# Maximum of three products as one product plus a clipped maximum of two difference products

## The chip, the cores and the metric

The kernel runs on one core of a Trainium2 chip. The metric is the device time of one execution in microseconds (us). The engines are called as in the profile: PE is the matrix engine (PEld its weight loads), DVE the vector engine, ACT the scalar engine, POOL GpSimd, SP the sync engine, which here issues loads and stores. The kernel has two parts in one launch: a gated linear attention, and behind it a feed-forward layer whose hidden values are a maximum of three products.

## The reference, cut to what matters

```python
# q, k, v, alpha: (4, 8, 768, 48) float32; w1, w2, w3: (384, 768); w_out: (768, 384)
for t in range(S):
    state = alpha[:, :, t, :, None] * state + einsum('bhd,bhe->bhde', k[:, :, t], v[:, :, t])
    y[:, :, t] = einsum('bhd,bhde->bhe', q[:, :, t], state)
x = y.transpose(0, 2, 1, 3).reshape(3072, 384)
h = np.maximum(np.maximum(x @ w1, x @ w2), x @ w3)
out = h @ w_out                                     # (3072, 384) float32
```

## The kernel before

**Groups.** The 3072 tokens are worked on in 12 groups of 256 (`n`; NG = 12, TG = 256). A group is two blocks of 128 tokens of one batch entry. Its attention takes two units `u`, four heads each; the feed-forward layer `ffn(n)` takes the whole group.

**Attention of a group.** SP loads a (alpha), q, k and v (`load`, L371) into one of five sets of buffers. `decay` makes logarithms of the decays on ACT (L402, L407; the product of two neighbouring decays before that is L398, on POOL for all but the first group). `prep` sums them with matmuls (L465, L468), takes exponentials on ACT (L473, L475), multiplies q and k by these (L482, mostly POOL) and scales v to f16 (L494). PE transposes q and k (L508), DVE copies them (L516), PE makes the scores (L528) and DVE masks them (L537). `state` sums the states (L560; L573, L579 and L447 carry them on), `output` adds the part from the state (L596) and from the scores (L617), ACT scales the result (L630), and PE turns it into `xT` (L638), which DVE (L649) or ACT (L645) copies. `xT`, f16, has x transposed: features on partitions, 256 tokens along the free axis, with 12 buffers, one per group.

**Feed-forward layer of a group.** `grow` takes two of the six blocks of 128 hidden features (`j`) and one of three weights (`g`): six matmuls of 128x128 weights with 256 columns of xT (L668), into one bank of PSUM. The first weight's product is copied to `hT` by ACT (L676); the second and third are taken in by DVE, as a maximum of the bank and hT (L680). `shrink` then multiplies six blocks of hT by Wout for each block of 128 tokens, 384 columns each (L692), ACT copies the result (L700) and SP stores it (L703). hT has three buffers, and the output four.

**Weights.** POOL's queue loads W1, W2 and W3 into `wcat` and Wout into `wo16`, turning them to f16 on the way (`weights`, L382). Each transfer has a gate, a step of the attention that must have come first (`WAFTER`): the first after v of unit 1, the second after v of unit 2, the third after k of unit 3, Wout after k of unit 5.

**What sets the order.** Nothing is scheduled by the compiler. Each piece of work is a step of a `Plan`, with its engine, an estimated cost, a rank, what it reads and writes and which of the eight PSUM banks it needs. `order` works through a list schedule on these estimates, with a model of the transfers: of all steps whose inputs, engine and banks are free, the one that can start earliest goes next, and the lower rank decides between equals. Attention steps have ranks near 2n, those of `ffn(n)` begin at 1.9n + 5.5. The instructions are then written in that order; each engine carries out its own in order and waits for what really has or has not come.

Of the kernel before, what the change touches and what calls it, by code (L numbers as in the profile page):

```python
# [10 lines left out]
FP32 = mybir.dt.float32  # L11
FP16 = mybir.dt.float16

AOP = mybir.AluOpType
AFT = mybir.ActivationFunctionType
# [6 lines left out]
NBANKS = 8  # L22
# [207 lines left out]
def kernel(  # L230
# [12 lines left out]
    nc = tc.nc  # L243

    B, H, S, D = q.shape
    NT, DM = out.shape
    DF = moe_w_out.shape[0]
    BH = B * H
    P = 128
# [4 lines left out]
    NFT = DM // P  # L254
    NJ = DF // P
    NU = NCB * B
    UB = 2
# [26 lines left out]
    sb = ctx.enter_context(tc.tile_pool(name="sb", bufs=1))  # L284
# [6 lines left out]
    ident, maskA, order = d16[:, :P], d16[:, P:3 * P], d16[:, 3 * P:]  # L291
# [7 lines left out]
    def homes(n, shape, dtype, name):  # L299
        return [sb.tile(shape, dtype, name=f"{name}{i}") for i in range(n)]  # L300
# [18 lines left out]
    e12s = homes(6, [P, NP, UB, 2], FP32, "e")  # L319
    G0s = homes(2, [P, NP], FP32, "G")  # L320
    G1s = homes(2, [P, NP], FP32, "H")
    wcat = sb.tile([P, NFT, 3, DF], FP16, name="wcat")
    wo16 = sb.tile([P, NJ, DM], FP16, name="wo16")
    for t in las:
        nc.vector.memset(t[:, :, :, D:], 0.0)
# [3 lines left out]
        for t in zz:  # L329
            nc.gpsimd.memset(t, 0.0)  # L330

    plan = Plan({x: range(NBANKS) for x in ("Lp", "hp", "tp", "A", "yp", "xp", "pp", "gp", "op")})
    place = {}

    psall = pspool.tile([P, NBANKS, 512], FP32, name="psum")
# [1 line left out]
    def bank(key, shape, dtype):  # L337
        n = int(np.prod(shape[1:]))
        flat = psall[:, place[key], :].bitcast(dtype) if dtype != FP32 else psall[:, place[key], :]
        if len(shape) == 3:  # L340
            return flat[:, :n].rearrange("p (a b) -> p a b", a=shape[1])
        if len(shape) == 4:
            return flat[:, :n].rearrange("p (a b c) -> p a b c", a=shape[1], b=shape[2])
        return flat[:, :n]
# [5 lines left out]
    live = {}  # L350
# [3 lines left out]
    LEAD = 5.5  # L354
    WAFTER = {2: (0,), 4: (1,), 7: (2,), 11: (3,)}
    SLOPE = 1.9
# [8 lines left out]
    def load(n, lo, hi, names="aqkv"):  # L365
        c, b = divmod(n, B)
        for x in names:
            t = ld[x][n % NL]

            def run(x=x, t=t):  # L370
                nc.sync.dma_start(t[:, lo:hi].rearrange("p h r d -> p h (r d)"),  # L371
                                  views[x][b, c][:, lo:hi])

            plan.step("SP", 0.5, -1.0, run, line="loads",
                      writes=[(x, n % NL, h) for h in range(lo // HH, hi // HH)],
                      load=LOAD * (hi - lo) / H)

    def weights(g, gate):
        w, dst = ((moe_w1, moe_w2, moe_w3, moe_w_out)[g],
                  wo16 if g == 3 else wcat[:, :, g, :])  # L380
        plan.step("POOL", 0.85, -1.0,
                  lambda: nc.gpsimd.dma_start(dst, w.rearrange("(t p) f -> p t f", p=P)),  # L382
                  reads=[gate], writes=[("w", g)], line="weights", load=3.25)


    def decay(n):
# [266 lines left out]
    def ffn(n):  # L653
        c, b = divmod(n, B)
        xT, hT = xTs[n], hTs[n % 3]
        npieces = 3 * (NJ // 2) + UB
        rank = [SLOPE * n + LEAD + SLOPE * i / npieces for i in range(npieces)]
        for j in range(NJ // 2):
            for g in range(3):
                r = rank[3 * j + g]  # L660
                gk = ("gp", n, j, g)

                def grow(j=j, g=g, gk=gk):
                    live[gk] = bank(gk, [P, 2, TG], FP32)
                    for jj in range(2):
                        c0 = (2 * j + jj) * P
                        for kt in range(NFT):
                            nc.tensor.matmul(live[gk][:, jj, :], wcat[:, kt, g, c0:c0 + P],  # L668
                                             xT[:, kt, :], start=(kt == 0), stop=(kt == NFT - 1))

                plan.step("PE", 0.656, r, grow, banks=[gk],
                          writes=[gk] + ([("room", n % 3, j)] if g == 0 else []),
                          reads=[("room", n % 3, j)] * (g > 0) + [("w", g), ("xT", n, 0), ("xT", n, 1)])
                h = hT[:, 2 * j:2 * j + 2, :]
                if g == 0:
                    plan.step("ACT", 0.59, r, lambda h=h, gk=gk: nc.scalar.copy(out=h, in_=live[gk]),  # L676
                              reads=[gk], writes=[("hT", n % 3, j)])
                else:
                    plan.step("DVE", 0.69, r,
                              lambda h=h, gk=gk: nc.vector.tensor_max(h, live[gk], h),  # L680
                              reads=[gk, ("hT", n % 3, j)], writes=[("hT", n % 3, j)])
        for i in range(UB):
            m = n * UB + i
            r = rank[3 * (NJ // 2) + i]
            ok = ("op", m)
            parts = [(0, NJ)] if n < NG - 1 else [(0, NJ - 2), (NJ - 2, NJ)]
            for lo, hi in parts:
                def shrink(i=i, ok=ok, lo=lo, hi=hi):
                    if lo == 0:
                        live[ok] = bank(ok, [P, DM], FP32)  # L690
                    for kt in range(lo, hi):
                        nc.tensor.matmul(live[ok], hT[:, kt, i * P:(i + 1) * P], wo16[:, kt, :],  # L692
                                         start=(kt == 0), stop=(kt == NJ - 1))

                plan.step("PE", 0.1627 * (hi - lo), r + (0.5 if lo else 0.0), shrink,
                          banks=[ok] if lo == 0 else [], writes=[ok, ("ob room", m % 4)],
                          reads=[(x, n % 3, j) for x in ("hT", "room")
                                 for j in range(lo // 2, hi // 2)]
                          + [("w", 3)])
            plan.step("ACT", 0.49, r, lambda m=m, ok=ok: nc.scalar.copy(out=obs[m % 4], in_=live[ok]),  # L700
                      reads=[ok], writes=[("ob", m % 4)])
            plan.step("SP", 0.4, -2.0,
                      lambda i=i, m=m: nc.sync.dma_start(  # L703
                          out[b * S + (2 * c + i) * P:b * S + (2 * c + i + 1) * P, :], obs[m % 4]),
                      reads=[("ob", m % 4), ("ob room", m % 4)], load=0.5)
# [5 lines left out]
    for n in range(NG):  # L711
        if n:
            load(n, 0, H)
        decay(n)
        for u in (2 * n, 2 * n + 1):
            prep(u)
            for j, key in ((2 * u, ("v16", u % NQ)), (2 * u + 1, ("qk", u % NQ, 1))):
                for g in WAFTER.get(j, ()):
                    weights(g, key)
        state(n)  # L720
        output(n)
        if n >= 4:
            ffn(n - 4)
    for n in range(NG - 4, NG):
        ffn(n)
# [35 lines left out]
```

## Time and profile before

| | |
|---|---|
| median of 3 runs | 165.33 us (164.88, 165.33, 165.47) |
| span of the profiled execution | 162.7 us; the runs' own times lie 2.2 to 2.8 us above it |
| PE busy | 146.5 us (90%), 2376 matmuls |
| DVE busy | 113.2 us (70%) |
| ACT busy | 84.5 us (52%) |
| POOL busy | 91.6 us (56%) |
| transfers | 26.50 MB, mean 163 GB/s |
| in the chain that ended last | PE 80% (L668 43%, L692 15%), DMA 8%, DVE 3% |

The span runs from the first to the last instruction; the page names no time for the profiled execution apart from the three runs. Busy time of PE counts each matmul to its modelled end, so neighbouring matmuls overlap in it; the spacing of matmuls is read from the chain of waits, where each piece begins when the one before it makes way. A digit of the rows of slices is a tenth of busy time in a fortieth of the span.

### The profile page before, as it was taken

The page shows a single profiled execution, that of the slowest core. Times are in us where ns is not written, and L with a number is a line of the kernel's source. Part 1 is how long each engine was busy: PE and PEld are TensorE (multiplying, and loading weights), DVE is VectorE, ACT ScalarE, POOL GpSimd, SP SyncE. Part 2 cuts the span into 40 slices and gives each one's busy share as a digit, 9 for nine tenths or more (in the row PEclk, how much of TensorE's full clock was granted, in tenths as well). Part 3 has the DMA queues.
Part 4 walks back from the last instruction along what each step waited for, and adds up shares of the span by engine and source line. Part 5 has one row for each costly group of instructions (what it writes and reads, how often), then busy time and mean ns, then how long its engine had stood idle before and what let it go on. Part 6 is the DMA issues. An engine that isn't in the chain of part 4 may idle for free.

```text
span 162.7 us, 5662 instructions
## 1 busy us (share of the span) xinstructions
PE 146.5 (90%) x2376; PEld 116.4 (72%) x2376; DVE 113.2 (70%) x172; ACT 84.5 (52%) x184; POOL 91.6 (56%) x145
## 2 busy tenths in 40 slices
PE   0279588998999999999999999999999999999990
PEld 0247356877787898887688886868868868878770
DVE  3458732899896789989389776558678678836460
ACT  3536327615775685465765755544634725363311
POOL 7087922934729999999569973482872652000000
PEclk9999999999999999999999999999999999999999
DMA  5999999999899989999999902311011020020202
GB/s 132 269 261 264 238 238 209 281 194 266 212 253 257 249 209 246 268 269 301 264 266 263 292 6 77 122 43 64 0 62 39 0 101 4 0 98 2 78 19 97
DMA packets 55880, 26.50 MB, mean 163 GB/s; under 512 B 50608, under 2 KB 55856, under 8 KB 55856
## 3 DMA queue, kind: packets, MB, share of 16 engines
q1 hardware_dynamic: 53440, 23.60, 58.7%
q0 software_dynamic: 1984, 2.36, 8.4%
q8 instruction: 18, 0.29, 0.8%
q10 hardware_dynamic: 432, 0.20, 0.7%
q14 instruction: 6, 0.05, 0.1%
HBM read 23.79 MB, written 4.72 MB: 175 GB/s over the span
## 4 chain that ended last, share of the span: by engine, by line
PE 80%; DMA 8%; DVE 3%; issue 2%; ACT 2%; POOL 2%; SPq 1%; ACTq 0%; DVEq 0%
PE psum L668 43%; PE psum L692 15%; DMA wcat<-in_moe_w_dram 5%; PE psum L528 4%; PE psum L508 4%; PE psum L617 3%; DMA an<-in_alpha_dram 3%; PE psum L638 3%; PE psum L560 3%; PE psum L465 2%; PE psum L596 2%; DVE LA L537 1%; DVE hT L680 1%; PE psum L468 1%; SPq L371 1%
## 5 line engine op out<-in xcount | busy, mean ns | idle before, releaser
L668 PE MATMUL psum<-xT,wcat 128*128 128x256 f16 x648 | 82.0, 276 | 2.0 <-DMA wcat<-in_moe_w_dram 2.0
L668 PEld LDWEIGHTS <-wcat 128*128 128x128 f16 x648 | 61.3, 99 | 10.4 <-DMA wcat<-in_moe_w_dram 2.1
L680 DVE TENSOR_TENSOR hT<-psum,hT 128x512 f16<-128x512 f32 x72 | 49.2, 689 | 23.9 <-PE psum L668 18.1
L676 ACT CAST hT<-psum 128x512 f16<-128x512 f32 x36 | 21.1, 587 | 27.1 <-PE psum L668 26.7
L537 DVE TENSOR_TENSOR LA<-psum,d 128x1024 f16<-128x1024 f32 x24 | 29.2, 1222 | 8.0 <-PE psum L528 7.1
L482 POOL TENSOR_TENSOR qk<-qn,ep 128x384 f16<-128x384 f32 x23 | 22.9, 998 | 17.6 <-ACT ep L473 11.3
L692 PE MATMUL psum<-wo,hT 128*128 128x384 f16 x144 | 26.3, 327 | 0.0
L482 POOL TENSOR_TENSOR qk<-kn,en 128x384 f16<-128x384 f32 x20 | 20.3, 1014 | 0.3
L700 ACT COPY ob<-psum 128x384 f32<-128x384 f32 x24 | 11.4, 478 | 15.1 <-PE psum L692 13.5
L692 PEld LDWEIGHTS <-hT 128*128 128x128 f16 x144 | 13.4, 98 | 7.7
L516 DVE COPY qkT<-psum 128x1024 f16<-128x1024 f16 x24 | 16.3, 683 | 1.9 <-PE psum L508 1.8
L473 ACT ACTIVATE ep<-psum 128x384 f32<-128x384 f32 x24 | 11.9, 494 | 9.9 <-PE psum L465 9.8
L494 POOL TENSOR_SCALAR v<-vn,c 128x384 f16<-128x384 f32 x23 | 13.4, 588 | 6.2 <-DMA vn<-in_v_dram 4.2
L630 ACT ACTIVATE xb<-psum,c 128x384 f16<-128x384 f32 x24 | 12.6, 576 | 5.9 <-PE psum L617 5.9
L465 PE MATMUL psum<-la,c 128*128 128x192 f16 x48 | 10.6, 262 | 5.5 <-ACT la L407 4.8
L447 POOL TENSOR_TENSOR Z<-U,G 48x192 f16<-48x192 f32 x16 | 8.0, 502 | 11.9 <-DVE U L573 11.2
L528 PE MATMUL psum<-qkT 48*64 48x128 f16 x384 | 10.9, 237 | 1.4 <-DVE qkT L516 1.4
L475 ACT ACTIVATE en<-psum 128x384 f32<-128x384 f32 x24 | 11.8, 493 | 0.0
L508 PE MATMUL psum<-d,qk 64*128 64x64 f16 x384 | 10.9, 199 | 0.3 <-POOL qk L482 0.3
L398 POOL TENSOR_TENSOR aa<-an 128x384 f32<-128x384 f32 x11 | 11.0, 1000 | 0.1
L528 PEld LDWEIGHTS <-qkT 48*64 48x64 f16 x384 | 6.7, 114 | 5.3 <-issue 2.4
L649 DVE CAST xT<-psum 128x384 f16<-128x384 f32 x12 | 6.6, 554 | 5.2 <-PE psum L638 5.0
(38 smaller groups left out, 135.8 us busy)
## 6 DMA issues: line engine op xcount, KB each, us to landing
out_dram<-ob SPq DMA_DIRECT2D x24, 192.0 KB, 2.1
an<-in_alpha_dram SPq DMA_DIRECT2D x11, 384.0 KB, 6.5
qn<-in_q_dram SPq DMA_DIRECT2D x11, 384.0 KB, 6.3
kn<-in_k_dram SPq DMA_DIRECT2D x11, 384.0 KB, 6.3
vn<-in_v_dram SPq DMA_DIRECT2D x11, 384.0 KB, 6.5
wcat<-in_moe_w_dram POOLq DMA_DIRECT2D x3, 576.0 KB, 8.2
wo<-in_moe_w_out_dram POOLq DMA_DIRECT2D x1, 576.0 KB, 9.4
an<-in_alpha_dram SPq DMA_DIRECT2D x2, 192.0 KB, 3.9
```

The costliest lines, as they stand in the source:

```text
L465: nc.tensor.matmul(live[Lk][:, :, r, :], tri, la[:, 0, hs, :D], start=True, stop=(r == 1))
L482: nc.gpsimd if eng == "POOL" else nc.vector).tensor_mul(
L494: lambda: nc.gpsimd.tensor_scalar(out=v16, in0=ld["v"][n % NL][:, hs], scalar1=vsc, scalar2=1.0, op0=AOP.mult, op1=AOP.mult),
L508: nc.tensor.transpose(live[tk][:, i, at:at + HALF], qk[rows, w, r, 2 * j:2 * j + 2, :], ident[rows, rows])
L516: lambda: nc.vector.tensor_copy(out=qkT.rearrange("p i w j t -> p i (w j t)"), in_=live[tk]),
L528: nc.tensor.matmul(live[Ak][i * HALF:(i + 1) * HALF, p, at:at + P], qkT[rows, i, 1, j, r * HALF:(r + 1) * HALF], qkT[rows, i, 0, j, :], st ...
L537: lambda: nc.vector.tensor_mul(LA.rearrange("p a j r t -> p (a j) (r t)"), live[Ak].rearrange("p a (j t) -> p (a j) t", j=2), maskA.unsque ...
L630: lambda xb=xb, yk=yk: nc.scalar.activation(out=xb, in_=live[yk].rearrange("p a b -> p (a b)"), func=AFT.Copy, scale=ysc),
L668: nc.tensor.matmul(live[gk][:, jj, :], wcat[:, kt, g, c0:c0 + P], xT[:, kt, :], start=(kt == 0), stop=(kt == NFT - 1))
L676: plan.step("ACT", 0.59, r, lambda h=h, gk=gk: nc.scalar.copy(out=h, in_=live[gk]), reads=[gk], writes=[("hT", n % 3, j)])
L680: lambda h=h, gk=gk: nc.vector.tensor_max(h, live[gk], h),
L692: nc.tensor.matmul(live[ok], hT[:, kt, i * P:(i + 1) * P], wo16[:, kt, :], start=(kt == 0), stop=(kt == NJ - 1))
```

## The change

With W1 in all three products, max(xW1, xW2, xW3) = xW1 + max(0, x(W2 - W1), x(W3 - W1)). The changed kernel makes the differences once, keeps max(0, ...) in hT, and takes xW1 through Wout as x(W1 Wout), where W1 Wout is made once on the chip:

- W1 has a tile of its own, `w1s`; W2 and W3 go to `wcat`, which has two parts now. `differences` subtracts W1 from each in place, in six steps on DVE, two blocks of 128 hidden features each; a grow piece waits for its own step.
- `bypass` transposes W1 on PE (18 blocks, three copies by ACT into `w1T`), multiplies by Wout (18 matmuls, three copies by ACT) and leaves the product in `past`. Both functions are called when the plan has come to group 3, with ranks of 5.0 to 6.5.
- A grow has two weights in place of three. The first product goes through Relu on ACT in place of the copy, the second into the maximum on DVE.
- A shrink begins with three matmuls of xT by `past` in the bank into which hT by Wout is summed. It waits for all of `past`.

```diff
--- before.py
+++ after.py
@@ -319,7 +319,10 @@
     e12s = homes(6, [P, NP, UB, 2], FP32, "e")
     G0s = homes(2, [P, NP], FP32, "G")
     G1s = homes(2, [P, NP], FP32, "H")
-    wcat = sb.tile([P, NFT, 3, DF], FP16, name="wcat")
+    w1s = sb.tile([P, NFT, DF], FP16, name="w1s")
+    w1T = sb.tile([P, NJ, DM], FP16, name="w1T")
+    past = sb.tile([P, NFT, DM], FP16, name="past")
+    wcat = sb.tile([P, NFT, 2, DF], FP16, name="wcat")
     wo16 = sb.tile([P, NJ, DM], FP16, name="wo16")
     for t in las:
         nc.vector.memset(t[:, :, :, D:], 0.0)
@@ -329,7 +332,7 @@
         for t in zz:
             nc.gpsimd.memset(t, 0.0)
 
-    plan = Plan({x: range(NBANKS) for x in ("Lp", "hp", "tp", "A", "yp", "xp", "pp", "gp", "op")})
+    plan = Plan({x: range(NBANKS) for x in ("Lp", "hp", "tp", "A", "yp", "xp", "pp", "gp", "op", "wt", "mp")})
     place = {}
 
     psall = pspool.tile([P, NBANKS, 512], FP32, name="psum")
@@ -377,10 +380,51 @@
 
     def weights(g, gate):
         w, dst = ((moe_w1, moe_w2, moe_w3, moe_w_out)[g],
-                  wo16 if g == 3 else wcat[:, :, g, :])
+                  (w1s, wcat[:, :, 0, :], wcat[:, :, 1, :], wo16)[g])
         plan.step("POOL", 0.85, -1.0,
                   lambda: nc.gpsimd.dma_start(dst, w.rearrange("(t p) f -> p t f", p=P)),
                   reads=[gate], writes=[("w", g)], line="weights", load=3.25)
+
+
+    def differences():
+        for g in range(2):
+            for j in range(NJ // 2):
+                cols = slice(2 * j * P, (2 * j + 2) * P)
+                plan.step("DVE", 0.47, LEAD - 0.5 + 0.5 * g,
+                          lambda g=g, cols=cols: nc.vector.tensor_sub(
+                              wcat[:, :, g, cols], wcat[:, :, g, cols], w1s[:, :, cols]),
+                          reads=[("w", 0), ("w", g + 1)], writes=[("d", g, j)])
+
+
+    def bypass():
+        rank = LEAD + 0.5 * SLOPE
+        for kt in range(NFT):
+            wk = ("wt", kt)
+
+            def turn(kt=kt, wk=wk):
+                live[wk] = bank(wk, [P, NJ, P], FP16)
+                for j in range(NJ):
+                    nc.tensor.transpose(live[wk][:, j, :], w1s[:, kt, j * P:(j + 1) * P], ident)
+
+            plan.step("PE", 0.36, rank, turn, banks=[wk], reads=[("w", 0)], writes=[wk])
+            plan.step("ACT", 0.82, rank,
+                      lambda kt=kt, wk=wk: nc.scalar.copy(
+                          out=w1T[:, :, kt * P:(kt + 1) * P], in_=live[wk]),
+                      reads=[wk], writes=[("w1T", kt)])
+        for kt in range(NFT):
+            mk = ("mp", kt)
+
+            def product(kt=kt, mk=mk):
+                live[mk] = bank(mk, [P, DM], FP32)
+                for j in range(NJ):
+                    nc.tensor.matmul(live[mk], w1T[:, j, kt * P:(kt + 1) * P], wo16[:, j, :],
+                                     start=(j == 0), stop=(j == NJ - 1))
+
+            plan.step("PE", 0.98, rank, product, banks=[mk], reads=[("w1T", kt), ("w", 3)],
+                      writes=[mk])
+            plan.step("ACT", 0.49, rank,
+                      lambda kt=kt, mk=mk: nc.scalar.copy(out=past[:, kt, :], in_=live[mk]),
+                      reads=[mk], writes=[("past", kt)])
 
 
     def decay(n):
@@ -653,11 +697,11 @@
     def ffn(n):
         c, b = divmod(n, B)
         xT, hT = xTs[n], hTs[n % 3]
-        npieces = 3 * (NJ // 2) + UB
+        npieces = 2 * (NJ // 2) + UB
         rank = [SLOPE * n + LEAD + SLOPE * i / npieces for i in range(npieces)]
         for j in range(NJ // 2):
-            for g in range(3):
-                r = rank[3 * j + g]
+            for g in range(2):
+                r = rank[2 * j + g]
                 gk = ("gp", n, j, g)
 
                 def grow(j=j, g=g, gk=gk):
@@ -670,10 +714,13 @@
 
                 plan.step("PE", 0.656, r, grow, banks=[gk],
                           writes=[gk] + ([("room", n % 3, j)] if g == 0 else []),
-                          reads=[("room", n % 3, j)] * (g > 0) + [("w", g), ("xT", n, 0), ("xT", n, 1)])
+                          reads=[("room", n % 3, j)] * (g > 0)
+                          + [("d", g, j), ("xT", n, 0), ("xT", n, 1)])
                 h = hT[:, 2 * j:2 * j + 2, :]
                 if g == 0:
-                    plan.step("ACT", 0.59, r, lambda h=h, gk=gk: nc.scalar.copy(out=h, in_=live[gk]),
+                    plan.step("ACT", 0.59, r,
+                              lambda h=h, gk=gk: nc.scalar.activation(out=h, in_=live[gk],
+                                                                      func=AFT.Relu),
                               reads=[gk], writes=[("hT", n % 3, j)])
                 else:
                     plan.step("DVE", 0.69, r,
@@ -681,22 +728,27 @@
                               reads=[gk, ("hT", n % 3, j)], writes=[("hT", n % 3, j)])
         for i in range(UB):
             m = n * UB + i
-            r = rank[3 * (NJ // 2) + i]
+            r = rank[2 * (NJ // 2) + i]
             ok = ("op", m)
             parts = [(0, NJ)] if n < NG - 1 else [(0, NJ - 2), (NJ - 2, NJ)]
             for lo, hi in parts:
                 def shrink(i=i, ok=ok, lo=lo, hi=hi):
                     if lo == 0:
                         live[ok] = bank(ok, [P, DM], FP32)
+                        for kt in range(NFT):
+                            nc.tensor.matmul(live[ok], xT[:, kt, i * P:(i + 1) * P],
+                                             past[:, kt, :], start=(kt == 0), stop=False)
                     for kt in range(lo, hi):
                         nc.tensor.matmul(live[ok], hT[:, kt, i * P:(i + 1) * P], wo16[:, kt, :],
-                                         start=(kt == 0), stop=(kt == NJ - 1))
-
-                plan.step("PE", 0.1627 * (hi - lo), r + (0.5 if lo else 0.0), shrink,
+                                         start=False, stop=(kt == NJ - 1))
+
+                plan.step("PE", 0.1627 * (hi - lo + (NFT if lo == 0 else 0)),
+                          r + (0.5 if lo else 0.0), shrink,
                           banks=[ok] if lo == 0 else [], writes=[ok, ("ob room", m % 4)],
                           reads=[(x, n % 3, j) for x in ("hT", "room")
                                  for j in range(lo // 2, hi // 2)]
-                          + [("w", 3)])
+                          + [("w", 3)]
+                          + ([("xT", n, i)] + [("past", kt) for kt in range(NFT)]) * (lo == 0))
             plan.step("ACT", 0.49, r, lambda m=m, ok=ok: nc.scalar.copy(out=obs[m % 4], in_=live[ok]),
                       reads=[ok], writes=[("ob", m % 4)])
             plan.step("SP", 0.4, -2.0,
@@ -719,6 +771,9 @@
                     weights(g, key)
         state(n)
         output(n)
+        if n == 3:
+            differences()
+            bypass()
         if n >= 4:
             ffn(n - 4)
     for n in range(NG - 4, NG):
```

## The prediction

> **What bounds the kernel now.** I read the page first: busy shares, the 40 slices, then the chain of waits, the groups by line, and the timelines of TensorE (PE) and GpSimd (POOL) around the first feed-forward matmuls. Whole lines of the page:
>
> ```profile
> PE 146.5 (90%) x2376; PEld 116.4 (72%) x2376; DVE 113.2 (70%) x172; ACT 84.5 (52%) x184; POOL 91.6 (56%) x145
> ...
> PE   0279588998999999999999999999999999999990
> ...
> DMA  5999999999899989999999902311011020020202
> ```
>
> A slice is 4.07 us. PE is full from the eleventh slice (about 41 us) to the end, while the transfers are full only until about 92 us: from 41 us on, what counts is the amount of PE work. The chain of waits says the same, and gives the rates:
>
> ```profile
> 12.53 8.23 DMA wcat<-in_moe_w_dram
> 20.80 1.46 PE psum L668 x6
> ...
> 40.35 1.04 PE psum L692 x6
> ...
> 137.04 0.34 PE psum L638 x6
> ...
> 144.34 6.55 PE psum L668 x60
> 150.89 1.95 PE psum L692 x12
> 152.84 3.93 PE psum L668 x36
> 156.77 1.64 PE psum L692 x10
> 158.48 0.28 ACT ob L700
> ```
>
> Full rates: L668 (x times W1/W2/W3, 256 columns) 6.55/60 = 0.109 us; L692 (times Wout, 384 columns) 1.95/12 = 0.1625 us; L638 (128 columns) 0.34/6 = 0.057 us. The first six L668, behind the landing of W1, took 1.46 us, more than twice the 0.655 us of later: PE is at half speed there. The last PE work ends at 158.4 us; 4.3 us of eviction and store follow, and the change leaves these alone.
>
> The stretch before 41 us decides what the change gives back. PE's timeline there (start, duration, ..., count):
>
> ```profile
> 20.80 1.46 PE L668 MATMUL psum<-xT,wcat 128*128 128x256 f16 x6 [1.96 <-DMA wcat<-in_moe_w_dram]
> 23.52 2.41 PE L668 MATMUL psum<-xT,wcat 128*128 128x256 f16 x12
> 28.05 0.82 PE L668 MATMUL psum<-xT,wcat 128*128 128x256 f16 x6
> 28.87 4.75 PE L668 MATMUL psum<-xT,wcat 128*128 128x256 f16 x42
> ```
>
> POOL's timeline and the view of the tile wcat date the landings:
>
> ```profile
> 18.34 1.59 POOL L382 DMA_DIRECT2D wcat<-in_moe_w_dram  x2
> 30.80 0.89 POOL L382 DMA_DIRECT2D wo<-in_moe_w_out_dram  x1
> ```
> ```profile
> DMA to landing us min/median/max: 8.1/8.2/10.9
> ```
>
> W1 lands at 12.53 + 8.2 = 20.8 us, W2 at 18.34 + 8.1 = 26.4, W3 (issued at 19.2) at 19.2 + 10.9 = 30.1, Wout at 30.8 + 9.4 = 40.2 (9.4 is its row among the DMA issues).
>
> **The change, part by part.**
>
> *Third product gone.* 36 grow pieces of 6 matmuls: 216 x 0.109 = 23.6 us of PE. With them go 36 of the 72 maxima on VectorE (DVE; L680, 689 ns): 24.8 us of DVE. DVE isn't the bound (70%), so that alone is worth nothing.
>
> *Shrink grows.* Three 384-column matmuls more for each of 24 outputs: 72 x 0.1625 = 11.7 us of PE.
>
> *The product W1 Wout.* 18 matmuls of 384 columns: 2.9 us. They need Wout, at 40.2 us, when PE is full: all on the path. The three evictions of 128x384 (478 ns at L700) hide under the next product; the first shrink, which waits for all of them, has other grow pieces beside it.
>
> *Transposes of W1.* 18 of 128 columns; nearest row L638: 18 x 0.057 = 1.0 us, twice that at half speed; the 64x64 transposes of L508 (0.34 us for 16) would make less. They can run from 20.8 us. From there to 26.4 us the changed kernel has no feed-forward matmul to run, so I cost them at nothing; if that cover is gone they cost 1.0 to 2.0 us. ScalarE (ACT) copies each of three 128x768 banks: from 482 ns for 384 and 587 for 512 columns (L645, L676), 0.82 ns a column, so 0.8 us each. Behind them in ACT's queue stands the logarithm L407 of the third group (22.78 us now, there behind an L676 that itself waited 3.2 us); I take that as even.
>
> *Differences.* Six DVE subtractions of 128x768 f16. No row has this form: the f32 128x384 product in SBUF takes 559 ns (L482 on DVE) and L680's 512 columns 689, 1.0 ns a column, which gives 0.94 us for 768; at the rate of the f16 copy L516, 1024 columns in 683 ns, it is 0.51. I take 0.7, the middle. In all 3 to 6 us of DVE, against 24.8 saved. On the path lies the first: the first grow piece now waits for W1, W2 and one subtraction, 26.4 + 0.7 = 27.1 us in place of 20.8. Behind waiting subtractions in DVE's queue stand the copies L516 and the masks L537 of the third group, and behind a waiting grow piece on PE the scores L528 and the rest of the attention.
>
> *Relu in place of the copy at L676.* Same shape, same engine. An Exp of 128x384 takes 494 ns against 482 for a cast: between nothing and 0.02 us each, on an engine that is 52% busy. Nothing.
>
> *Queues.* SP and POOL get no new instruction; the transfers of the weights keep their gates, though the planner may order things anew around them.
>
> *The late start.* By 40.25 us PE has now run 96 L668 (10.5 us): groups 0 and 1, 54 each, are nearly used up, and the third group's xT is copied only at 43.4 us (DVE's timeline). In the changed kernel these two groups hold 72 matmuls (7.9 us), and from 27.1 to 40.25 us are 13.1 us in which to run them and the 3.6 us that a group's attention takes (its pieces in the chain added up). They fit, but there are no more: 24 x 0.109 = 2.6 us of PE work less is done by then, whatever idles. If the third group's attention comes earlier, as a DVE with six maxima fewer by then may let it, this term falls to zero.
>
> *The clock.* The half speed ended at 25.8 us, five us after PE's dense work began. If it lasts five us from 27.1 instead, 2.5 us of work is lost; the window has 13.1 - 11.5 = 1.6 us to spare, so the excess is 0.9, and 2.5 if attention fills that. I take 0, since transposes and attention now fill 20.8 to 27.
>
> The sum: -23.6 + 11.7 + 2.9 + 2.6 = -6.4 us. Against the profiled span, 162.7 becomes 156.3; the span stands 2.6 us below the median of the runs, 165.33, and with the same 2.6 us around it the time is 158.9.
>
> On the clock a rule speaks against this change. The Trainium skill, in "TensorE: Matmul & The Clock Gate" (Part 4, PE-mode transpose), says that the full clock doesn't engage for transposes, because they don't count as PE activity; by it the transposes between 20.8 and 27 us would do nothing for the first grow pieces, and the sum would be -6.4 + 2.5, or 161.4 us. The trace bears out the half speed (1.46 against 0.655 us) but has no such transposes.
>
> **The rivals.**
>
> *A late and slow start.* PE stays at half speed until 32 us or so (2.5 us) and the transposes are not hidden (up to 1.0): 158.9 + 2.5 to 3.5, some 161.8. For it: PE was busy 7.8 us between 10 and 20 us without leaving half speed, since that work had gaps. Against it: the attention of the second group fills much of 20.8 to 27 in any case, at half speed all the more.
>
> *The gap costs nothing.* Attention takes the place of the early grow pieces, the third group's xT comes by about 37 us: 165.33 - 9.0 = 156.3. For it: L528 at 22.19 us stood behind the L668 that waited 1.96 us for W1. Against it: v of the third group was issued at 16.06 us and landed 14.5 us later (DMA issues of that stretch), at 30.6, which bounds how early that attention can be.
>
> *A blocked queue.* Orders are written from planned landings, and W1's came at least 1.96 us later than planned. If all six subtractions stand in DVE's queue ahead of the third group's copies and wait for W3, grow pieces and attention start near 31 us: four us more, and the cold start's 2.5 on top undo the 6.4: 165.3, on either side of no change. It decides only if the planner puts W3's landing some 4 us too early; W2 and W3 show no wait now.
>
> *Slower: Relu makes ACT reload its table.* One ACT_TABLE_LOAD is in the trace, 1283 ns, for Exp, Ln and Copy together. If Relu sat in another table, each of 36 would cost up to two loads between Exp and Ln: 92 us, and ACT would hold 84.5 + 3.9 + 92 = 181 us of work, a time of some 183. It decides from (155 - 88)/1.283 = 52 loads. Against it: three functions share one load already. The Trainium skill, "ScalarE: Activation LUTs" (Table sets: the hidden batching unit), counts relu among the functions that appear in every set, which would rule it out; no run here shows a Relu yet.
>
> **How the numbers follow.** Forecast 0.62; late and slow start 0.17; the gap costs nothing 0.11; blocked queue 0.07; table reloads 0.03. A measurement of this kernel can tell some 0.5% (0.8 us) from no change. The first three are faster: 0.90. The blocked queue splits 0.04 same and 0.03 slower, the reloads are slower: 0.06. The range leaves out the last two and the outer edges of the others: from 156.4, where nothing is lost at the start, to 162.2, where half speed and most of the transposes count. The forecast is the likeliest case's 158.9.
>
> **What would show it.** PE still full from about 41 us to the end, its chain at 0.109 and 0.1625 us a matmul; 432 L668, 216 matmuls in the shrink; the first grow piece at 27 us and six of them either 0.66 or 1.46 us long, which decides the clock; transposes between 20.8 and 27 us; the products soon after Wout's landing near 40; ACT with one table load; the third group's xT earlier than 43.4 us or not. PE with idle tenths after 41 us would prove the argument wrong, as would a VectorE or ScalarE wait taking PE's place in the chain.

## The result, and the profile after

The changed kernel takes 157.88 us (median; 157.0 to 159.75), against 165.31 us in the same measurement: a ratio of 0.9548, interval 0.9501 to 0.9596. A second measurement on the chip of the experiments gave 158.69 us against 164.87, 0.9628 (0.9580 to 0.9676). The gain is 6.2 to 7.4 us; 6.4 were forecast, at 158.9 us. The execution profiled below took 159.75 us, the longest of its set; its span is 157.1.

The page of the changed kernel, the rows that answer to those of before:

```profile
PE 138.8 (88%) x2268; PEld 105.2 (67%) x2268; DVE 95.4 (61%) x142; ACT 88.0 (56%) x190; POOL 92.5 (59%) x145
...
PE   0278558897999999999999999999999999999990
...
PEclk9999956999999999999999999999999999999999
DMA  5999999999999999998999990222011002011112
```

PE's row is full from about 41 us to the end as before; the slices of 20 to 40 us are emptier. DVE fell by 18 us. PEclk shows half speed between 20 and 27 us here and none before, although the first six grow matmuls took 1.46 us there and later sixes 0.66. The row does not show every stretch at half speed, so the speed is read below from the matmuls' own times, and from the granted clock only where these agree with it.

Its chain of waits (L407 are the transposes of W1, L394 the subtractions, L712 the grow pieces, L420 the product W1 Wout, L739 and L742 the shrink's matmuls by that product and by Wout):

```profile
12.27 8.94 DMA w1s<-in_moe_w_dram
21.25 1.46 PE psum L407 x12
...
28.41 1.82 DVE wcat L394 x2
30.23 1.27 DVE qk L526
31.50 3.01 DVE wcat L394 x2
34.55 1.49 PE psum L712 x12
...
41.56 0.97 PE psum L420 x6
...
140.48 4.59 PE psum L712 x42
145.06 0.49 PE psum L739 x3
145.55 0.97 PE psum L742 x6
```

The rates are those of before: 4.59/42 = 0.109 us and (0.49 + 0.97)/9 = 0.162 us a matmul. What is new is VectorE in the chain from 28.4 to 34.5 us; before, it stood there between 33.0 and 38.4 us. PE's timeline of that stretch:

```profile
28.21 1.64 PE L712 MATMUL psum<-xT,wcat 128*128 128x256 f16 x12
30.28 2.79 PE L712 MATMUL psum<-xT,wcat 128*128 128x256 f16 x24 [0.44 <-DVE wcat L394]
...
33.58 2.45 PE L712 MATMUL psum<-xT,wcat 128*128 128x256 f16 x18
...
36.54 0.83 PE L712 MATMUL psum<-xT,wcat 128*128 128x256 f16 x6
...
39.92 1.47 PE L712 MATMUL psum<-xT,wcat 128*128 128x256 f16 x12
```

The first grow piece starts at 28.2 us, at full speed already, and 60 grow matmuls (12 + 24 + 18 + 6) are behind PE when the last row begins. Before, 96 were by then. 36 x 0.109 = 3.9 us of work are still to do. Set against the 9.0 us of PE work that the change takes out (-23.6 + 11.7 + 2.9), that leaves 5.1; PE's last end moved from 158.4 to 153.2 us, 5.2. So the profile's ledger closes.

### The profile page after: what moved, and what is told of

Same layout as the page of the kernel before. It is cut to its first block, busy times and chain, and to the rows that moved or that the text cites. A ratio compares the mean times of both kernels' runs of the same rounds, so it can differ in the third digit from the quotient of the medians.

```text
span 157.1 us, 5400 instructions
## 1 busy us (share of the span) xinstructions
PE 138.8 (88%) x2268; PEld 105.2 (67%) x2268; DVE 95.4 (61%) x142; ACT 88.0 (56%) x190; POOL 92.5 (59%) x145
## 4 chain that ended last, share of the span: by engine, by line
PE 77%; DMA 8%; DVE 7%; issue 2%; POOL 2%; ACT 1%; SPq 1%; ACTq 0%; DVEq 0%
PE psum L712 27%; PE psum L742 15%; PE psum L739 8%; DMA w1s<-in_moe_w_dram 6%; PE psum L572 5%; PE psum L661 4%; PE psum L552 3%; DVE wcat L394 3%; DMA an<-in_alpha_dram 3%; PE psum L509 3%; PE psum L604 3%; PE psum L682 2%; PE psum L640 2%; PE psum L420 2%; DVE LA L581 2%
## 5 line engine op out<-in xcount | busy, mean ns | idle before, releaser
L712 PE MATMUL psum<-xT,wcat 128*128 128x256 f16 x432 | 54.1, 273 | 0.6 <-DVE wcat L394 0.4
L712 PEld LDWEIGHTS <-wcat 128*128 128x128 f16 x432 | 40.0, 98 | 6.7 <-DVE wcat L394 1.4
L727 DVE TENSOR_TENSOR hT<-psum,hT 128x512 f16<-128x512 f32 x36 | 24.4, 687 | 15.0 <-PE psum L712 13.6
L722 ACT ACTIVATE hT<-psum 128x512 f16<-128x512 f32 x36 | 21.4, 597 | 14.4 <-PE psum L712 13.7
L742 PE MATMUL psum<-wo,hT 128*128 128x384 f16 x144 | 27.3, 326 | 0.0
L742 PEld LDWEIGHTS <-hT 128*128 128x128 f16 x144 | 14.1, 98 | 9.3
L509 PE MATMUL psum<-la,c 128*128 128x192 f16 x48 | 11.2, 272 | 6.2 <-ACT la L451 4.8
L739 PE MATMUL psum<-past,xT 128*128 128x384 f16 x72 | 15.6, 326 | 0.0
L674 ACT ACTIVATE xb<-psum,c 128x384 f16<-128x384 f32 x24 | 12.6, 579 | 3.1 <-PE psum L661 3.0
L572 PE MATMUL psum<-qkT 48*64 48x128 f16 x384 | 10.1, 232 | 1.4 <-DVE qkT L560 1.4
L552 PE MATMUL psum<-d,qk 64*128 64x64 f16 x384 | 10.4, 196 | 0.8 <-POOL qk L526 0.8
```

Of the source, the lines that this page charges most:

```text
L509: nc.tensor.matmul(live[Lk][:, :, r, :], tri, la[:, 0, hs, :D], start=True, stop=(r == 1))
L552: nc.tensor.transpose(live[tk][:, i, at:at + HALF], qk[rows, w, r, 2 * j:2 * j + 2, :], ident[rows, rows])
L572: nc.tensor.matmul(live[Ak][i * HALF:(i + 1) * HALF, p, at:at + P], qkT[rows, i, 1, j, r * HALF:(r + 1) * HALF], qkT[rows, i, 0, j, :], st ...
L722: lambda h=h, gk=gk: nc.scalar.activation(out=h, in_=live[gk], func=AFT.Relu),
L739: nc.tensor.matmul(live[ok], xT[:, kt, i * P:(i + 1) * P], past[:, kt, :], start=(kt == 0), stop=False)
```

## The experiments

Theory: behind 41 us the amount of PE work sets the time, and the late start gives some back. First rival: the gain comes through VectorE's relief. Later rivals concern what sets the start.

**The changed kernel again**, for a second profile.

> The changed kernel itself, for a second profile and a closer time. Theory (the amount of PE work behind 41 us sets the time; the start gives back 1 to 4 us, more or less by when the half speed ends): 157 to 159 us, 0.950 to 0.962 of before, first grow piece between 27 and 28.5 us. Rival (the time follows VectorE's load, which fell by 18 us of busy time): the same time; this run does not separate them.

Measured: 158.69 us, 0.9628 (0.9580 to 0.9676); the first grow piece at 28.4 us, PE's last end at 153.45. As expected.

**Without the product W1 Wout.**

```diff
+    nc.gpsimd.memset(past, 0.0)
...
-        for kt in range(NFT):
-            mk = ("mp", kt)
-
-            def product(kt=kt, mk=mk):
...
```

> Leaves out the 18 matmuls of W1 Wout and their copies; the product is zeros, so xW1 is missing from the output. Theory of PE work: they cost 18 x 0.1625 = 2.9 us on a full PE, so this is 2.5 to 3.2 us under the changed kernel, about 154.9. Rival (VectorE): PE between 41 and 50 us waits for other things anyway and the time stays within 0.5 us of the changed kernel's.

Measured: 157.61 us, 0.9563 (0.9526 to 0.9600), 1.1 us under the changed kernel's second measurement; PE's last end is 1.4 us earlier. Less than the theory's 2.9, more than the rival's 0.5. Where the rest went shows in the windows of 50 to 90 us (start and end, length, then PE's busy time), with the product and without:

```profile
50.00:90.00 40.00, 39.88 (x728) 30.96 (x726) 26.06 (x38) 27.56 (x62) 35.80 (x57) 1.00 1.09 258
```
```profile
50.00:90.00 40.00, 38.94 (x736) 30.99 (x734) 28.11 (x40) 27.09 (x63) 37.78 (x60) 1.00 1.08 259
```

With 2.9 us less to do, PE idles 0.9 us longer while q, k and v are still arriving. The order has changed too: shrinks, which wait for no product now, run from 41.5 us on, and the third group's xT is copied at 47.6 us in place of 44.9. The remaining half microsecond isn't located.

**Without the shrink's three matmuls.**

```diff
-                        for kt in range(NFT):
-                            nc.tensor.matmul(live[ok], xT[:, kt, i * P:(i + 1) * P],
-                                             past[:, kt, :], start=(kt == 0), stop=False)
...
```

> Makes the product W1 Wout, but leaves the three matmuls of xT by it out of every shrink: 72 x 0.1625 = 11.7 us of PE less, while VectorE and ScalarE have the same work. Theory of PE work: 11.0 to 11.9 us under the changed kernel, about 146.3, if PE stays full behind 41 us. Rival (VectorE or the transfers carry the time, or become the bound as PE shrinks): under 6 us less.

Measured: 148.75 us, 0.9007 (0.8955 to 0.9060): 9.9 us less for 11.7 us of PE work. Between theory and rival, near the theory: 85% of the PE work taken away comes out of the time. The rival's less than 6 us falls.

**Before, with VectorE relieved alone.**

```diff
-                else:
+                elif g == 1:
                     plan.step("DVE", 0.69, r,
                               lambda h=h, gk=gk: nc.vector.tensor_max(h, live[gk], h),
```

> The kernel before with all its products, but the third one's maximum left out (W3's product is made and dropped): 36 x 0.69 = 24.8 us of VectorE less, PE the same. Theory of PE work: the time of before, 164.3 to 165.3, at most 0.5 us from VectorE's stretch between 32 and 39 us. Rival (the change gains through VectorE's relief): most of the change's gain, 159 to 161.

Measured: 165.21 us, 1.0001 (0.9973 to 1.0029). 23 us of VectorE's busy time less are worth nothing by themselves; the first rival falls.

**Before, without the third product.**

```diff
-            for g in range(3):
-                r = rank[3 * j + g]
+            for g in range(2):
+                r = rank[2 * j + g]
...
```

> The kernel before with the third product left out altogether and nothing put in its place: 216 matmuls, 23.6 us of PE less, and no differences, no product, no late start. Theory of PE work: 23.6 us less, 141.7, or some 1.5 us above that, as the run without xW1's three matmuls gave 10 of 11.7 us, because PE then waits between 50 and 90 us. The changed kernel less the three matmuls (148.8) holds 2.9 us of product besides, so what is left between the two, 2.5 to 4.5 us, is the price of the late start. Rival (transfers or the attention become the bound): over 146.

Measured: 147.05 us, 0.8884 (0.8830 to 0.8938): 18.4 of 23.6 us by the ratio (18.2 by the medians), and not the 141.7 of the theory; the time is on the rival's side. PE's timeline shows the first place:

```profile
40.04 0.59 PE L617 MATMUL psum<-v,LA 64*128 64x48 f16 x32
41.88 2.08 PE L692 MATMUL psum<-wo,hT 128*128 128x384 f16 x6 [1.25 <-DMA wo<-in_moe_w_out_dram]
```

The 72 grow matmuls of the first two groups are used up by 36 us, PE waits for Wout and is at half speed after it: 2.08 us for six matmuls that take 1.14 elsewhere. The mean granted clock is 0.973 in this profile and 0.988 in the run's other executions, so the half speed lasts longer here than usual. PE idles again between 60 and 70 us, where it is busy 8.57 of 10 us. So the price of the late start can't be read off by setting this run against the one without the shrink's three matmuls, as I had meant to: it has a price of its own, of the same kind.

**The same, with POOL relieved.**

```diff
     EARLY = {...
+             **{u: ("POOL", "DVE", "POOL") for u in range(9, 24, 2)}}
```

> The run without the third product (no_third, 147.05, where 23.6 us of PE work less gave 18.2), with the product of k moved from POOL to VectorE in every second unit from the ninth on: POOL was 96% to 97% busy there between 60 and 100 us, and stood in the chain of waits. Theory (POOL paces the attention once PE has work to spare): 1 to 3 us less, 144 to 146, and PE fuller between 60 and 90 us. Rival (the transfers pace it until 92 us): within 0.7 us of no_third.

Measured: 0.8969 (0.8897 to 0.9041), no gain over 0.8884. The theory falls: with POOL's busy time down from 91.4 to 85.8 us, PE still idles between 60 and 70 us (busy 7.66 of 10). VectorE took over the work and is busy 8.92 us there in place of 7.39; that it took POOL's place as the limit isn't ruled out. That the transfers pace it, full until about 92 us in all these runs, fits but was not isolated.

**No subtractions.**

```diff
-                          + [("d", g, j), ("xT", n, 0), ("xT", n, 1)])
+                          + [("w", 0), ("w", g + 1), ("xT", n, 0), ("xT", n, 1)])
...
-            differences()
```

> Leaves out the six subtractions; a grow piece waits for W1 and its own weight only. The output is that of undiminished W2 and W3. In the profile of the changed kernel they take 6.3 us of VectorE between 26.7 and 36.2 us, one of them 2.6 us, and the first grow piece starts at 28.2. Theory that they hold VectorE's queue, and with it the third group's attention and PE until 40 us: 1.5 to 3 us under the changed kernel, first grow piece at 26.5 to 27.2 us, xT of the third group over 1.5 us earlier than 44.6. Rival (the start is bound by the landings alone, and the subtractions are beside that): within 0.8 us of the changed kernel.

Measured: 157.53 us, 0.9560 (0.9513 to 0.9607), 1.2 us under the changed kernel, with overlapping intervals; the first grow piece at 27.84, the third group's xT at 44.39. Neither: the subtractions cost something like a microsecond, but the start hardly moves, since the piece stands in PE's queue behind the second group's turning (L682, which waits 0.67 us for ACT's L674). What moves is the stretch behind it. PE's timeline ends it with

```profile
37.91 1.47 PE L712 MATMUL psum<-xT,wcat 128*128 128x256 f16 x12
...
40.37 1.14 PE L420 MATMUL psum<-wo,w1T 128*128 128x384 f16 x6 [0.81 <-DMA wo<-in_moe_w_out_dram]
```

With the first of these rows all 72 grow matmuls of the first two groups are done (6 + 36 + 12 + 6 + 12), by 39.2 us, where the changed kernel has done 60 by 39.9. Then the product waits 0.8 us for Wout.

**The first group with three products.**

```diff
+        G = 2 if n else 3
+        ws = [wd[:, :, 0, :], wd[:, :, 1, :]] if n else [w1s, wcat[:, :, 0, :], wcat[:, :, 1, :]]
...
-                          + [("d", g, j), ("xT", n, 0), ("xT", n, 1)])
+                          + [("d", g, j) if n else ("w", g), ("xT", n, 0), ("xT", n, 1)])
```

> The changed kernel, but the first group still takes three products of W1, W2 and W3 as they are, with differences in a tile of their own; it has no matmul by W1 Wout. PE gets 18 x 0.109 - 6 x 0.1625 = 1.0 us more work and DVE three maxima more, but the first grow piece needs W1 alone and starts at 21.3 in place of 28.3 us. Theory (late start): 18 matmuls, 2.0 us, move into the gap, 1 to 2 us net of the 1.0, so 0.5 to 2 us under the changed kernel. Rival (VectorE's queue between 28 and 38 us sets the start): same as the changed kernel or up to 1.5 us more.

Measured: 161.24 us, 0.9767 (0.9733 to 0.9801): 2.3 us over the changed kernel by the ratios, 2.6 by the medians. The grow pieces do start at 21.45 us, and it is slower all the same, more than the rival said. PE then waits for VectorE with the third group's attention:

```profile
37.18 0.39 PE L553 MATMUL psum<-d,qk 64*128 64x64 f16 x15 [1.19 <-DVE hT L730]
...
41.22 0.41 PE L553 MATMUL psum<-d,qk 64*128 64x64 f16 x16 [0.88 <-DVE LA L582]
```

**v of two units on ScalarE.**

```diff
-             5: ("POOL", "DVE", "POOL"), ...
+             4: ("POOL", "POOL", "ACT"), 5: ("POOL", "DVE", "ACT"), ...
```

> The changed kernel, with v of units 4 and 5 scaled on ScalarE and no longer on POOL. In the profile of the changed kernel one subtraction of 0.55 us took 2.6, from 31.4 to 34.1 us, while POOL worked on these two v (31.97 to 33.1) and on the next decays (to 34.07). Theory (a subtraction with two operands in SBUF and a POOL operation shut each other out): the long subtraction ends with POOL's last operation, over 0.8 us earlier, and the time falls by 0.3 to 1 us. Rival (the subtraction waits for W3's data or for PE): it stays over 2 us long at the same place.

Measured: 158.45 us, 0.9607 (0.9565 to 0.9649), which the intervals don't separate from the changed kernel. On the mechanism the theory holds. VectorE's and POOL's timelines of the changed kernel:

```profile
28.41 1.82 DVE L394 TENSOR_TENSOR wcat<-wcat,w1s 128x768 f16<-128x768 f16 x2
...
31.42 3.07 DVE L394 TENSOR_TENSOR wcat<-wcat,w1s 128x768 f16<-128x768 f16 x2
...
35.61 0.55 DVE L394 TENSOR_TENSOR wcat<-wcat,w1s 128x768 f16<-128x768 f16 x1
```
```profile
31.97 1.14 POOL L538 TENSOR_SCALAR v<-vn,c 128x384 f16<-128x384 f32 x2
33.08 0.99 POOL L442 TENSOR_TENSOR aa<-an 128x384 f32<-128x384 f32 x1
```

and of this run:

```profile
31.18 1.01 DVE L394 TENSOR_TENSOR wcat<-wcat,w1s 128x768 f16<-128x768 f16 x2
```
```profile
32.29 0.99 POOL L442 TENSOR_TENSOR aa<-an 128x384 f32<-128x384 f32 x1 [0.61 <-DVE wcat L394]
```

The pair falls from 3.07 to 1.01 us, and POOL's next operation now waits for VectorE. The Trainium skill, in "SBUF — State Buffer" (Who interferes with whom), says that a vector instruction with two SBUF inputs contends with a GpSimd instruction that reads SBUF. Both rows agree with it. One thing is open: the long subtraction's record begins at 31.4 us, half a microsecond before the first v, and yet it ends with POOL's last operation.

**Weights earlier**, in the changed kernel, with v on ScalarE too, and in the kernel before.

```diff
-    WAFTER = {2: (0,), 4: (1,), 7: (2,), 11: (3,)}
+    WAFTER = {0: (0,), 2: (1,), 4: (2,), 9: (3,)}
```

> The changed kernel with the gates of the weights' transfers two or more steps earlier (W1 after v of unit 0, W2 after v of unit 1, W3 after v of unit 2, Wout after k of unit 4), so W1 is issued about 4 us earlier. Theory (the first grow piece waits for W2, and that costs PE time before 41 us): W2 lands near 23, the first grow starts at 23.5 to 25 in place of 28.3, and the time falls by 1 to 2.5 us against the changed kernel's 0.963 of before, to 0.95 or so. Rival (VectorE's queue with the third group's attention sets the start, and the transfers of q, k and v come as much later): within 0.5 us of the changed kernel, or slower by up to 1.

> The same earlier gates, and v of units 4 and 5 on ScalarE as in v_on_act. Theory: 0 to 1 us under early_w, since VectorE's subtractions are no longer drawn out by POOL when its queue is what the third group waits for. Rival: like early_w.

> The kernel before with the same earlier gates, to see whether they help without the change. Before, the first grow waits for W1 alone, at 20.8 us; earlier it finds only the first group's xT, ready at about 18.7 us. Theory: within 0.8 us of before, 0.995 to 1.005. Rival: as much gain as in early_w.

Measured: 1.0034 (1.0000 to 1.0069), 0.9959 (0.9921 to 0.9996) and 1.0237 (1.0188 to 1.0286) of before. The first and the third theory fell. The first one's rival had the direction and underrated it: the whole gain is gone. In the second the order of the two held, 1.2 us under the first by the ratios (165.32 and 164.48 us by the medians), on a lost base. In the first of them the first grow piece starts six microseconds earlier, and then PE runs dry. PE's timeline and the windows of 20 to 40 us (after POOL's busy time: granted clock, transfers' share):

```profile
22.25 3.73 PE L712 MATMUL psum<-xT,wcat 128*128 128x256 f16 x18 [3.27 <-DVE wcat L394]
...
32.19 0.97 PE L682 MATMUL psum<-d,xb 128*128 128x128 f16 x6 [0.67 <-ACT xb L674]
```
```profile
20.00:30.00 10.00, 6.35 (x108) 4.61 (x109) 5.84 (x9) 5.65 (x12) 5.64 (x6) 0.83 1.16 252
30.00:40.00 10.00, 7.18 (x134) 4.89 (x134) 8.56 (x13) 3.10 (x7) 5.86 (x8) 0.62 1.10 237
```

The second group's turning (L682) comes at 32.2 us in place of 27.6. Its v is late: POOL waits 1.00 us for it and scales it from 21.96 us on, in place of 16.61. And in PE's queue its attention stands behind the 18 grow matmuls, which themselves wait 3.27 us for the first subtraction. The two causes weren't separated. W3, whose gate stands behind v of unit 2 in POOL's queue, is issued at 24.22 us in place of about 19. PE does 18 matmuls at half speed, then idles, and the granted clock is 0.62 of full between 30 and 40 us. The kernel before loses 4 us by the same edit; there the rival, a gain, was wrong as well.

No run that makes the whole output beat the changed kernel clear of its interval. Giving W1 for transposing to ordinary matmuls, to see what that does to the clock, was not tried.

## Why the prediction was right, point by point

*The sum* was -23.6 + 11.7 + 2.9 + 2.6 = -6.4 us, and the runs gave -6.2 and -7.4. Its signs and its ground, PE's work behind 41 us, held: fewer maxima alone gave nothing, and taking PE's matmuls away shortens the time. That the total came out so near is in part luck. Set in a row, the run without the third product, the one without the shrink's three matmuls and the changed kernel measure 0.8884, 0.9007 and 0.9628 of before. That is 18.4 us saved where the sum had 23.6, then some 2 us for the product, the subtractions and the late start where it had 5.5, then some 10 us for the shrink's matmuls where it had 11.7. The saving was over-rated by about 5 us, and the costs by about as much.

*The PE terms* are right in the profile (same rates, full row), but a microsecond of PE work isn't quite a microsecond of time. The 11.7 us measured 9.9 by leaving them out, the 2.9 us 1.1, and the 23.6 us 18.4. In every case PE idles somewhere before 90 us for what it no longer has to do. I had said that PE is full and left unsaid how near it is to running out of work while q, k and v arrive.

*The late start* was under-sized: 2.6 us forecast, 3.9 by the count of matmuls in the profile. The start was put at 27.1 us and came at 28.2: W2's first subtraction ends at 27.5 us, but the piece stands behind the second group's turning. The step that failed is "they fit": 72 matmuls should have been done by 40.25 us, and 60 were by 39.9. What took the place is the subtractions in VectorE's queue. Without them all 72 are done by 39.2 us; the 12 matmuls are 1.3 us of work, and that run is 1.2 us shorter, though its interval overlaps. VectorE's queue was nearly full before as well. The windows of 30 to 40 us, before and after (VectorE's busy time is the third after the length):

```profile
30.00:40.00 10.00, 9.38 (x154) 7.86 (x152) 9.44 (x15) 4.03 (x9) 4.88 (x7) 1.00 1.21 240
```
```profile
30.00:40.00 10.00, 8.31 (x139) 6.58 (x140) 10.00 (x13) 4.79 (x10) 4.02 (x5) 1.00 1.10 214
```

In place of some of the maxima it now holds subtractions, and copies and masks of the third group stand behind these, as the prediction said without putting a price on it.

*The subtractions* were put at 0.7 us each between bounds of 0.51 and 0.94. The view of the line gives 545, 690 and 2604 ns as the least, the median and the most: alone near the lower bound, beside POOL far outside both. In all 6.3 us, just above "3 to 6".

*The transposes* ran between 21.25 and 24.8 us at half speed. Whether they hid, as costed, was not tested: 2.2 us of them are in the chain of waits, ahead of the second group's attention and so of the first grow piece. They can have held that piece up by at most 0.7 us, an estimate from the end of W2's first subtraction at 27.5 us and the start at 28.2.

*The clock* was taken at nothing; it was full at 26.7 us, 1.2 us later than before (25.5 us, by the twelve grow matmuls at 23.52 us that took 2.41), and the first grow piece ran at full speed. So the 161.4 us by the Trainium skill's rule on transposes did not come about here; that rule itself isn't refuted, since attention matmuls ran in the same stretch. The late and slow start did appear, in the runs with earlier weights.

*Relu* cost 597 ns against 587, and the trace has one table load, 1283 ns, as before. The reload rival falls.

*The gap costs nothing*: no. The third group's xT is copied on VectorE at 44.6 us, later than the 43.4 of before.

*A blocked queue*: VectorE stands in the chain for 8.6 of the 11.3 us from 28.4 to 39.7 us, by its own work and by POOL's beside it, not by waiting for W3.

The profile's own difference, 5.2 us by PE's last end, is below that of the runs. Executions of the changed kernel spread over some 2 us (spans 155.2 to 157.5) where those of before spread over 1.8 (162.0 to 163.8); what moves them is open, the granted clock doesn't order them.

## What to carry to other kernels

When an engine is full, cost a change by its work at the rates of the chain, but look for the stretch where the full engine is about to run out of supply: there, work taken away turns into waiting. A new step ahead of the first use of a tensor is costed by the queue that it joins, and whose work stands behind it, more than by its own duration. Moving the weights' transfers earlier while the transfers were saturated came with a later v here; find out who needs the other transfers first.

## What the runs showed of the hardware that was not expected

A 128x768 f16 subtraction with both operands in SBUF takes 0.55 us alone and up to 2.6 us beside POOL's operations on SBUF; POOL's 128x384 product of q went from 1.00 to 1.38 us beside it. Either can be the one that waits: in one run VectorE's subtraction lasted through three POOL operations, in another POOL waited 0.6 us for VectorE. And an early start can cost speed: with the weights earlier, the 18 matmuls at 22.25 us ran at half speed, and after the gaps that followed, none of them over 1.35 us, PE was at half speed again from about 32.4 to 42.6 us, where the changed kernel runs at full speed from 26.7 us on. How much of the lost gain this makes up was not isolated.
